# Moving the query transposes of an attention-then-FFN kernel from TensorE to the DMA crossbar, in a layout where two neighbouring tokens share the partitions

## The chip, the cores and the metric

The kernel runs on one core of one Trainium2 chip. The metric is the device time of that core in microseconds (us). Each kernel was run on the same chip beside the kernel before. "Span" is the length of the profiled execution, about 1.8 us shorter than the time. "Granted clock" is the TensorE clock that the profile shows as granted, as a share of full speed.

In this kernel TensorE does the matmuls and, before the change, all transposes; VectorE and ScalarE copy, scale and combine its results; SyncE and GpSimd (POOL) issue the DMAs. SBUF is the on-chip memory that the loads fill, PSUM the one that TensorE writes to. A crossbar transpose is a DMA instruction (`dma_start_transpose`) that writes what it reads transposed.

## The reference

Linformer attention over 8 batches, 8 heads, 1024 tokens and head width 64, followed by a gated FFN over all 8192 tokens:

```python
k_proj = np.einsum('ks,bhsd->bhkd', E, k)          # 1024 tokens -> 64 rows
v_proj = np.einsum('ks,bhsd->bhkd', F, v)
scores = scale * np.matmul(q, k_proj.transpose(0, 1, 3, 2))
attn = exp(scores) / sum(exp(scores))               # the kernel leaves the maximum out
x = np.matmul(attn, v_proj)                         # -> (8192, 512)
gate = 1.0 / (1.0 + np.exp(-(x @ w_gate)))
out = (gate * (x @ w_val)) @ w_out                  # d_ff = 1536, all arrays float32
```

## The kernel before

A small planner records every operation with the tiles it reads and writes; each engine then runs its own list in order and waits on semaphores only. TensorE runs the FFN of batch b and, woven in between, the "pieces" of the attention of batch b + 1.

```python
        def load_kvq(b):                     # POOL queue; casts float32 to bf16 on the way
            s = b % 2
            for t, d, n in ((Kb, k, "K"), (Vb, v, "V"), (Qb, q, "Q")):
                load(t[s][:, :, :],
                     d[b].rearrange("h (p t) d -> p h (t d)", t=NT), [(n, s)], f"{n}{s}")
            # partition p holds tokens 8p .. 8p+7 of each head; t is the token in it
# ... cut ...
            def qt(r):                       # transpose the queries of heads 2r and 2r+1
                bk = next_bank()
                ob = bank[bk][:, :].bitcast(BF16)
                for t in range(NT):
                    for h in range(2):       # 16 transposes in 128x64 tiles
                        mm(bk, ob[64 * h : 64 * h + 64, t * P : (t + 1) * P],
                           Qb[s][:, 2 * r + h, t * DH : (t + 1) * DH],
                           ident[:, :], [("Q", s), "ident"], tr=True, tp=(0, 64 * h))
                dve(lambda e: e.tensor_copy(qT[:, r, :], ob[:, :]), [], [("qT", r)], b=bk)
# ... cut: sc(r) two scores of heads 2r, 2r+1; den, rec, split: 1/sum; bc(c): broadcast it ...
            def xo(c):                       # output: block-diagonal V of two heads
                r, hf = c // 2, c % 2
                bk = next_bank()
                mm(bk, bank[bk][:, :], vpBD[:, r, :], aT[c % 2][:, :], [...])
                act(xT[s][:, r, hf * 512 : (hf + 1) * 512], bank[bk][:, :], [], [...], b=bk)
# ... cut ...
        for piece in attention(0):
            piece()
        load_kvq(1)
        load(wO[:, :, :], moe_w_out.rearrange("(m p) c -> p m c", p=P), ["wO"], "wO")
        for b in range(B):
            pieces = attention(b + 1) if b + 1 < B else []
            todo = list(slots(b))            # 24 FFN steps, and 8 output blocks (4 in batch 0)
            n, done = len(todo) - 1, 0
            for i, slot in enumerate(todo):
                slot()
                while done < len(pieces) and done * n < (i + 1) * len(pieces):
                    pieces[done](); done += 1
            # ... cut: the rest of the pieces; load_kvq(b + 2) ...
```

The attention of batch 0 comes before the first FFN step. Weights and inputs all pass through one load queue, in the order K, V, Q of batch 0, the gate and value weights, K, V, Q of batch 1, wO, K, V, Q of batch 2.

The softmax here doesn't subtract the row's maximum and nothing guards it: scores larger than these inputs give would overflow.

Of the kernel before, what the change touches and what calls it, by code (L numbers as in the profile page):

```python
# [7 lines left out]
ALU = mybir.AluOpType  # L8
# [4 lines left out]
P = 128  # L13
# [106 lines left out]
def bass_linformer_attn__then__ffn_glu_sigmoid_kernel(  # L120
# [18 lines left out]
    with contextlib.ExitStack() as es:  # L139
# [28 lines left out]
        kpBD = sbuf("kpBD", [P, NR, P], BF16)  # L168
        vpBD = sbuf("vpBD", [P, NR, P], BF16)
        qT = sbuf("qT", [P, NR, S], BF16)  # L170
        eT = sbuf("eT", [P, NR, 2, 512], BF16)
        aT = [sbuf(f"aT{i}", [P, 512], BF16) for i in range(2)]
# [3 lines left out]
        xT = [sbuf(f"xT{i}", [P, NI, S], BF16) for i in range(2)]  # L176
# [62 lines left out]
        def constants():  # L239
# [9 lines left out]
            pool(lambda e: e.memset(kpBD[:, :, :], 0.0), w=["kpBD0", "kpBD1"])  # L249
            pool(lambda e: e.memset(vpBD[:, :, :], 0.0), w=["vpBD0", "vpBD1"])  # L250
# [84 lines left out]

        def attention(b):
# [3 lines left out]
            def kv():  # L340
                bk = next_bank()
                for src, wt, c0, n in ((Kb[s], ET, 0, "K"), (Vb[s], FT, 256, "V")):
                    sv = src[:, :, :].rearrange("p (r h) (t d) -> p h t r d", h=2, t=NT)
                    for t in range(NT):
                        for h in range(2):
                            mm(
                                bk,
                                bank[bk][64 * h : 64 * h + 64, c0 : c0 + 256],
                                wt[:, t, :],
                                sv[:, h, t, :, :],  # L350
                                [(n, s), ("ET" if n == "K" else "FT")],
                                start=(t == 0),
                                stop=(t == NT - 1),
                                tp=(0, 64 * h),
                            )
                act(kp[:, :, :], bank[bk][:, 0:256], [], ["kp"], b=bk)
                for h in range(2):
                    hh = slice(64 * h, 64 * h + 64)
                    act(
                        vpBD[hh, :, hh],  # L360
                        bank[bk][hh, 256:512].rearrange("p (r d) -> p r d", r=NR),
                        [],
                        [f"vpBD{h}"],
                        b=bk,
                    )

            def kt():
                bk = next_bank()
                ob = bank[bk][:, :].bitcast(BF16)
                for r in range(NR):  # L370
                    for h in range(2):
                        mm(
                            bk,
                            ob[64 * h : 64 * h + 64, r * P : (r + 1) * P],
                            kp[:, r, :],
                            ident[:, :],
                            ["kp", "ident"],
                            tr=True,
                            tp=(0, 64 * h),
                        )  # L380
                for h in range(2):
                    hh = slice(64 * h, 64 * h + 64)
                    act(
                        kpBD[hh, :, hh],
                        ob[hh, 0:512].rearrange("p (r c) -> p r c", r=NR)[:, :, hh],
                        [],
                        [f"kpBD{h}"],
                        b=bk,
                    )

            def qt(r):
                bk = next_bank()
                ob = bank[bk][:, :].bitcast(BF16)
                for t in range(NT):
                    for h in range(2):
                        mm(
                            bk,
                            ob[64 * h : 64 * h + 64, t * P : (t + 1) * P],
                            Qb[s][:, 2 * r + h, t * DH : (t + 1) * DH],
# [3 lines left out]
                            tp=(0, 64 * h),  # L403
                        )
                dve(lambda e: e.tensor_copy(qT[:, r, :], ob[:, :]), [], [("qT", r)], b=bk)  # L405

            def sc(r):
                for hf in range(2):
                    bk = next_bank()
                    mm(  # L410
                        bk,
                        bank[bk][:, :],
                        kpBD[:, r, :],
                        qT[:, r, hf * 512 : (hf + 1) * 512],
                        ["kpBD0", "kpBD1", ("qT", r)],
                    )
                    act(
                        eT[:, r, hf, :],
                        bank[bk][:, :],
                        [],  # L420
                        [("eT", r, hf)],
                        b=bk,
                        func=AF.Exp,
                        scale=SCALE,
                    )

            def den():
                bk = next_bank()
                st["den"] = bk
                for rnd in range(2):  # L430
                    for j in range(4):
                        r, hf = 2 * rnd + j // 2, j % 2
# [4 lines left out]
                            eT[:, r, hf, :],  # L437
                            ["dsel", ("eT", r, hf)],
# [26 lines left out]
            def bc(c):  # L465
                r, hf = c // 2, c % 2
                rnd, j = r // 2, 2 * (r % 2) + hf
                bk = next_bank()
                mm(bk, bank[bk][:, :], bsel[:, j, rnd, :], rhl[:, :], ["bsel", "rhl"])
                dve(  # L470
                    lambda e: e.tensor_tensor(  # L471
                        aT[c % 2][:, :], eT[:, r, hf, :], bank[bk][:, :], ALU.mult
                    ),
                    [("eT", r, hf)],
                    [("aT", c % 2)],
# [3 lines left out]
            def xo(c):  # L479
                r, hf = c // 2, c % 2  # L480
                bk = next_bank()
                mm(
                    bk,
                    bank[bk][:, :],
                    vpBD[:, r, :],
                    aT[c % 2][:, :],
                    ["vpBD0", "vpBD1", ("aT", c % 2)],
                )
                act(
                    xT[s][:, r, hf * 512 : (hf + 1) * 512],  # L490
                    bank[bk][:, :],
                    [],
                    [("xT", s, r, hf)],
                    b=bk,
                )

            out = [kv, lambda: qt(0), kt, lambda: qt(1)]
            out += [lambda: sc(0), lambda: qt(2), lambda: sc(1), lambda: qt(3)]
            out += [lambda: sc(2), lambda: sc(3), den]
            out += [lambda c=c: rec(c) for c in range(4)] + [split]  # L500
            out += [lambda: bc(0)]
            for c in range(1, 8):
                out += [lambda c=c: (bc(c), xo(c - 1))]
            out += [lambda: xo(7)]
# [5 lines left out]
        def mstep(blk, m):  # L510
# [3 lines left out]
            for W, pb, n in ((wG, PG[M % 2], "wG"), (wV, PV[M % 2], "wV")):  # L514
                for i in range(NI):
# [4 lines left out]
                        xT[s][:, i, hf * 512 : (hf + 1) * 512],  # L520
# [28 lines left out]
        def oproj(blk, tt, pb):  # L549
            T = 4 * blk + tt  # L550
            for m in range(NF):
# [18 lines left out]
                lambda e: e.dma_start(out_v[blk // 2, 4 * (blk % 2) + tt], o[:, :]),  # L570
# [18 lines left out]
        load_kvq(1)  # L589
        load(wO[:, :, :], moe_w_out.rearrange("(m p) c -> p m c", p=P), ["wO"], "wO")  # L590
        for b in range(B):
# [6 lines left out]
            n, done = len(todo) - 1, 0  # L598
            for i, slot in enumerate(todo):
                slot()  # L600
                while done < len(pieces) and done * n < (i + 1) * len(pieces):
# [5 lines left out]
            if load_next is not None:  # L607
                load_kvq(load_next)
# [33 lines left out]
```

## Time and profile before

| | before |
|---|---|
| time, median (range) of the 4 runs | 628.91 us (628.47 to 630.4) |
| period of a full batch on TensorE | 73.11 us |
| one group of query transposes, as delay of the next FFN matmul | 0.654 us |
| four groups a batch, seven batches | 18.3 us |

From the page of the kernel before: its span, the busy row of TensorE and the chain of work that ended last, by engine and by line.

```profile
span 627.3 us, 8171 instructions
PE 589.8 (94%) x3344; PEld 274.7 (44%) x3408; DVE 275.8 (44%) x413; ACT 204.5 (33%) x363; POOL 32.4 (5%) x60
...
PE 88%; DMA 6%; POOL 2%; DVE 2%; issue 1%; ACT 1%; DVEq 0%; POOLq 0%
```

TensorE (PE) is the bound. The 6% of DMA are the load of batch 1's queries at the start, which landed at 54.0 us.

From TensorE's timeline before: start, length, instruction and count. The first three lines are one query group between two FFN matmul groups; the last three show the old output product between a broadcast and the FFN.

```profile
189.33 1.03 PE L202 MATMUL pV<-xT,wV 128*128 128x512 bf16 x4
190.28 0.64 PE L202 MATMUL pA<-ident,Qb 128*64 128x128 bf16 x16
190.85 1.04 PE L202 MATMUL pG<-xT,wG 128*128 128x512 bf16 x4
...
161.67 0.38 PE L202 MATMUL pA<-rhl,bsel 128*128 128x512 bf16 x1
161.89 0.38 PE L202 MATMUL pA<-aT,vpBD 128*128 128x512 bf16 x1
162.10 1.03 PE L202 MATMUL pG<-xT,wG 128*128 128x512 bf16 x4
```

Lengths include the pipeline's tail, so read starts. A 512-column matmul starts 0.216 us after the one before it (161.67, 161.89, 162.10). Four of them from 189.33 end their turn at 190.196; the next FFN matmul starts at 190.85. The query group therefore costs 0.654 us.

From the same timeline, the first projection of K in the attention of batches 1, 2 and 7, which mark where the batches begin:

```profile
45.58 1.06 PE L202 MATMUL pA<-Kb,ET 128*64 128x256 bf16 x16
113.47 1.06 PE L202 MATMUL pA<-Kb,ET 128*64 128x256 bf16 x16
479.02 1.06 PE L202 MATMUL pA<-Kb,ET 128*64 128x256 bf16 x16
```

The period is (479.02 - 113.47) / 5 = 73.11 us.

### The profile page before, as it was taken

To read this page: it belongs to the slowest core of one execution; us is meant where nothing else is said; L and a number is where in the kernel's file an instruction comes from. 1 tells how busy PE (TensorE), PEld (TensorE's weight loads), DVE (VectorE), ACT (ScalarE), POOL (GpSimd) and SP (SyncE) were. 2 spreads that over 40 slices of the span, in tenths; PEclk is the share of its full clock that TensorE was granted. 3 is DMA by queue.
4 is the path that set the end of the run, shared out by engine and by line. 5 is a ranking of instruction groups with operands and counts; after the bars stand their busy time and mean duration, and the time that the engine had idled before them with its cause. 6 is when DMAs were issued, how large, how long until landed. Compare 5 with 4: busy or idle time off the path is not lost.

```text
span 627.3 us, 8171 instructions
## 1 busy us (share of the span) xinstructions
PE 589.8 (94%) x3344; PEld 274.7 (44%) x3408; DVE 275.8 (44%) x413; ACT 204.5 (33%) x363; POOL 32.4 (5%) x60
## 2 busy tenths in 40 slices
PE   2558999999999999999999999999999999999997
PEld 1313444544444444544445444444445444444443
DVE  2162465336543365334653365433653346533332
ACT  1333424232333324333242323333243332422220
POOL 8301000100001000100001000000000000000000
PEclk9978999999999999999999999999999999999999
DMA  9999990652009500375006620000000000000002
GB/s 138 207 207 207 207 175 34 113 106 67 34 35 152 101 34 19 63 138 85 34 34 111 114 62 34 34 18 33 34 24 27 34 18 34 34 34 33 34 33 84
DMA packets 39092, 47.44 MB, mean 76 GB/s; under 512 B 1552, under 2 KB 30736, under 8 KB 39056
## 3 DMA queue, kind: packets, MB, share of 16 engines
q0 software_dynamic: 29840, 30.15, 30.4%
q1 hardware_dynamic: 9216, 16.78, 7.2%
q8 instruction: 26, 0.43, 0.3%
q14 instruction: 10, 0.08, 0.0%
HBM read 60.29 MB, written 16.78 MB: 123 GB/s over the span
## 4 chain that ended last, share of the span: by engine, by line
PE 88%; DMA 6%; POOL 2%; DVE 2%; issue 1%; ACT 1%; DVEq 0%; POOLq 0%
PE pG L202 26%; PE pO L202 25%; PE pV L202 25%; PE pA L202 12%; DMA Qb<-in_q_dram 6%; DVE ost L563 1%; DVE aT L471 1%; ACT sig L206 1%; POOL wG L221 0%; POOL dsel L258 0%; POOL wV L221 0%; POOL Kb L221 0%; POOL Vb L221 0%; POOL bsel L251 0%; POOL Qb L221 0%
## 5 line engine op out<-in xcount | busy, mean ns | idle before, releaser
L536 DVE SCALAR_TENSOR_TENSOR hT<-sig,pV 128x512 bf16<-128x512 f32 x192 | 132.1, 688 | 211.4 <-PE pV L202 207.2
L202 PE MATMUL pG<-xT,wG 128*128 128x512 bf16 x750 | 195.4, 380 | 2.2 <-issue 1.4
L202 PE MATMUL pV<-xT,wV 128*128 128x512 bf16 x746 | 195.7, 380 | 0.8
L206 ACT ACTIVATE sig<-pG 128x512 f32<-128x512 f32 x192 | 114.8, 598 | 246.1 <-PE pG L202 231.7
L202 PE MATMUL pO<-wO,hT 128*128 128x512 bf16 x717 | 166.1, 379 | 2.3 <-issue 1.0
L202 PEld LDWEIGHTS pV<-xT,wV 128*128 128x128 bf16 x768 | 75.4, 98 | 91.2 <-issue 1.1
L202 PEld LDWEIGHTS pG<-xT,wG 128*128 128x128 bf16 x768 | 72.2, 98 | 88.2 <-issue 4.4
L202 PEld LDWEIGHTS pO<-wO,hT 128*128 128x128 bf16 x732 | 70.6, 98 | 85.8 <-DVE ost L563 1.3
L563 DVE TENSOR_SCALAR ost<-pO 128x512 f32<-128x512 f32 x61 | 42.2, 692 | 104.4 <-PE pO L202 104.4
L206 ACT ACTIVATE xT<-pA 128x512 bf16<-128x512 f32 x64 | 38.3, 598 | 68.2 <-PE pA L202 68.0
L206 ACT ACTIVATE eT<-pA 128x512 bf16<-128x512 f32 x64 | 34.7, 596 | 48.5 <-PE pA L202 48.5
L471 DVE TENSOR_TENSOR aT<-eT,pA 128x512 bf16<-128x512 bf16 x64 | 43.5, 681 | 2.1 <-PE pA L202 2.0
L448 DVE RECIPROCAL rden<-pA 128x128 f32<-128x128 f32 x32 | 30.0, 946 | 2.1 <-PE pA L202 2.1
L405 DVE COPY qT<-pA 128x1024 bf16<-128x1024 bf16 x32 | 22.1, 690 | 18.2 <-PE pA L202 18.2
L202 PE MATMUL pA<-rhl,bsel 128*128 128x512 bf16 x58 | 23.0, 400 | 6.2 <-DVE rhl L458 5.0
L202 PE MATMUL pA<-ident,Qb 128*64 128x128 bf16 x512 | 21.5, 229 | 4.3 <-DMA Qb<-in_q_dram 4.0
L202 PE MATMUL pA<-aT,vpBD 128*128 128x512 bf16 x63 | 24.4, 387 | 0.8 <-DVE aT L471 0.7
L202 PEld LDWEIGHTS pA<-ident,Qb 128*64 128x64 bf16 x512 | 16.2, 114 | 18.4 <-issue 11.4
L202 PE MATMUL pA<-qT,kpBD 128*128 128x512 bf16 x63 | 19.1, 384 | 0.8 <-ACT kpBD L206 0.5
L221 POOL DMA_DIRECT2D Kb<-in_k_dram x8 | 7.2, 899 | 217.6 <-PE pA L202 217.6
L202 PE MATMUL pA<-Kb,ET 128*64 128x256 bf16 x128 | 9.4, 294 | 6.7 <-DMA Kb<-in_k_dram 6.7
L202 PE MATMUL pA<-Vb,FT 128*64 128x256 bf16 x128 | 9.2, 292 | 5.5 <-DMA Vb<-in_v_dram 5.5
(53 smaller groups left out, 119.3 us busy)
## 6 DMA issues: line engine op xcount, KB each, us to landing
out_dram<-ost SPq DMA_DIRECT2D x64, 256.0 KB, 2.0
Kb<-in_k_dram POOLq DMA_DIRECT2D x8, 1024.0 KB, 9.8
Vb<-in_v_dram POOLq DMA_DIRECT2D x8, 1024.0 KB, 14.6
Qb<-in_q_dram POOLq DMA_DIRECT2D x8, 1024.0 KB, 13.9
wG<-in_moe_w_gate_dram POOLq DMA_DIRECT2D x3, 512.0 KB, 19.4
wV<-in_moe_w_val_dram POOLq DMA_DIRECT2D x3, 512.0 KB, 21.2
wO<-in_moe_w_out_dram POOLq DMA_DIRECT2D x1, 1536.0 KB, 44.3
Ebf<-in_E_dram POOLq DMA_DIRECT2D x1, 128.0 KB, 2.9
```

What stands on the lines that cost most here:

```text
L202: return add("PE", lambda e: e.matmul(o, lhsT, rhs, **kw), r=r, x=[("bank", b)])
L206: return add("ACT", lambda e: e.activation(o, i, func, scale=scale), r=r, w=w, x=x)
L221: add("POOL", lambda e: e.dma_start(o, i), r=r, w=w, dma=sem)
L405: dve(lambda e: e.tensor_copy(qT[:, r, :], ob[:, :]), [], [("qT", r)], b=bk)
L448: lambda e: e.reciprocal(rden[:, cc], bank[bk][:, cc]),
L471: lambda e: e.tensor_tensor(aT[c % 2][:, :], eT[:, r, hf, :], bank[bk][:, :], ALU.mult),
L536: lambda e: e.scalar_tensor_tensor(hT[blk % 2][:, m, :], sg[:, :], 1.0, bank[PV[M % 2]][:, :], ALU.add, ALU.mult,),
L563: lambda e: e.tensor_scalar(o[:, :], bank[pb][:, :], 0.5, None, op0=ALU.mult),
```

## The change

The intent is to take the query transposes, and the copies out of PSUM behind them, off the compute engines. Batches 1 to 7 get their transposed queries from four crossbar transposes each, issued on SyncE's queue from SBUF to SBUF. Such a transpose turns 128 columns of Qb at a time into 128 partitions, and 128 columns are two neighbouring tokens of 64 values: so the transposed queries of the even tokens lie in partitions 0 to 63 and those of the odd tokens in 64 to 127. The rest of the attention follows this layout: one head per score matmul, K twice on a diagonal, and the output product as four 64x64 tiles. Batch 0 keeps TensorE, with eight full 128x128 transposes per group.

```diff
+        def transpose_q(b):
+            s = b % 2
+            for r in range(NR):
+                add(
+                    "SP",
+                    lambda e, r=r: e.dma_start_transpose(
+                        qT[s][:, 2 * r : 2 * r + 2, :].rearrange("p h (t c) -> p (h t) c", c=P),
+                        Qb[s][:, 2 * r : 2 * r + 2, :].rearrange("p h c -> p (h c)"),
+                    ),
+                    r=[("Q", s)], w=[("qT", s, r)], dma=f"qT{s}{r}",
+                )
@@ qt: groups of transposes, now for batch 0 only @@
-                for t in range(NT):
-                    for h in range(2):
+                for h in range(2):
+                    for t in range(4):
...
-                            Qb[s][:, 2 * r + h, t * DH : (t + 1) * DH],
+                            Qb[s][:, 2 * r + h, t * P : (t + 1) * P],
@@ the output product @@
-            def xo(c):   # one 128x128 matmul per half, into one bank
+            def xo(r):
+                bks = [next_bank(), next_bank()]
+                for g in range(2):
+                    gg = slice(64 * g, 64 * g + 64)
+                    for c in range(2):
+                        h = 2 * r + c
+                        mm(bks[g], bank[bks[g]][64 * c : 64 * c + 64, :],
+                           vpD[gg, h, :], aT[h % 4][gg, :],
+                           [("vpD", c, g), ("aT", h % 4)], tp=(64 * g, 64 * c))
@@ the order @@
         load_kvq(1)
+        transpose_q(1)
         load(wO[:, :, :], moe_w_out.rearrange("(m p) c -> p m c", p=P), ["wO"], "wO")
...
+            if load_next is not None:
+                load_kvq(load_next)
             for i, slot in enumerate(todo):
                 slot()
+                if i == 16 and load_next is not None:
+                    transpose_q(load_next)
... (cut: the tiles' shapes, sc, den and bc by head, the evictions of K and V, the rows of the output)
```

More of the change, by code (lines that the diff above doesn't have):

```diff
@@ L167, in bass_linformer_attn__then__ffn_glu_sigmoid_kernel @@
         kp = sbuf("kp", [P, NR, DH], BF16)
-        kpBD = sbuf("kpBD", [P, NR, P], BF16)
-        vpBD = sbuf("vpBD", [P, NR, P], BF16)
-        qT = sbuf("qT", [P, NR, S], BF16)
-        eT = sbuf("eT", [P, NR, 2, 512], BF16)
-        aT = [sbuf(f"aT{i}", [P, 512], BF16) for i in range(2)]
+        kpBD = sbuf("kpBD", [P, H, P], BF16)
+        vpD = sbuf("vpD", [P, H, DH], BF16)
+        qT = [sbuf(f"qT{i}", [P, H, 512], BF16) for i in range(2)]
+        eT = sbuf("eT", [P, H, 512], BF16)
+        aT = [sbuf(f"aT{i}", [P, 512], BF16) for i in range(4)]
         rden = sbuf("rden", [P, 512], FP32)
@@ L175, in bass_linformer_attn__then__ffn_glu_sigmoid_kernel @@
         rhl = sbuf("rhl", [P, 512], BF16)
-        xT = [sbuf(f"xT{i}", [P, NI, S], BF16) for i in range(2)]
+        xT = [sbuf(f"xT{i}", [P, NI, 2, 512], BF16) for i in range(2)]
         wG = sbuf("wG", [P, NI, DFF], BF16)
@@ L248, in constants @@
             )
-            pool(lambda e: e.memset(kpBD[:, :, :], 0.0), w=["kpBD0", "kpBD1"])
-            pool(lambda e: e.memset(vpBD[:, :, :], 0.0), w=["vpBD0", "vpBD1"])
+            pool(lambda e: e.memset(kpBD[:, :, :], 0.0), w=[("kpBD", 0), ("kpBD", 1)])
             pool(lambda e: e.memset(bsel[:, :, :, :], 0.0), w=["bsel"])
@@ L334, in next_bank @@
             return b
+        def transpose_q(b):
[7 more added lines that the diff above has]
+                    ),
+                    r=[("Q", s)],
+                    w=[("qT", s, r)],
+                    dma=f"qT{s}{r}",
+                )
         def attention(b):
@@ L356, in kv @@
                 act(kp[:, :, :], bank[bk][:, 0:256], [], ["kp"], b=bk)
+                vv = vpD[:, :, :].rearrange("p (r h) d -> p r h d", h=2)
                 for h in range(2):
-                    hh = slice(64 * h, 64 * h + 64)
-                    act(
-                        vpBD[hh, :, hh],
-                        bank[bk][hh, 256:512].rearrange("p (r d) -> p r d", r=NR),
-                        [],
-                        [f"vpBD{h}"],
-                        b=bk,
-                    )
+                    for g in range(2):
+                        act(
+                            vv[64 * g : 64 * g + 64, :, h, :],
+                            bank[bk][64 * h : 64 * h + 64, 256:512].rearrange(
+                                "p (r d) -> p r d", r=NR
+                            ),
+                            [],
+                            [("vpD", h, g)],
+                            b=bk,
+                        )
             def kt():
@@ L370, in kt @@
                 for r in range(NR):
-                    for h in range(2):
+                    for g in range(2):
                         mm(
                             bk,
-                            ob[64 * h : 64 * h + 64, r * P : (r + 1) * P],
+                            ob[64 * g : 64 * g + 64, r * P : (r + 1) * P],
                             kp[:, r, :],
@@ L378, in kt @@
                             tr=True,
-                            tp=(0, 64 * h),
+                            tp=(0, 64 * g),
                         )
-                for h in range(2):
-                    hh = slice(64 * h, 64 * h + 64)
-                    act(
-                        kpBD[hh, :, hh],
-                        ob[hh, 0:512].rearrange("p (r c) -> p r c", r=NR)[:, :, hh],
+                for g in range(2):
+                    gg = slice(64 * g, 64 * g + 64)
+                    act(
+                        kpBD[gg, :, gg],
+                        ob[gg, 0:512].rearrange("p (h c) -> p h c", h=H),
                         [],
-                        [f"kpBD{h}"],
+                        [("kpBD", g)],
                         b=bk,
@@ L393, in qt @@
                 ob = bank[bk][:, :].bitcast(BF16)
-                for t in range(NT):
-                    for h in range(2):
-                        mm(
-                            bk,
-                            ob[64 * h : 64 * h + 64, t * P : (t + 1) * P],
-                            Qb[s][:, 2 * r + h, t * DH : (t + 1) * DH],
+                for h in range(2):
+                    for t in range(4):
+                        c = h * 4 + t
+                        mm(
+                            bk,
+                            ob[:, c * P : (c + 1) * P],
+                            Qb[s][:, 2 * r + h, t * P : (t + 1) * P],
                             ident[:, :],
@@ L402, in qt, with sc @@
                             tr=True,
-                            tp=(0, 64 * h),
                         )
-                dve(lambda e: e.tensor_copy(qT[:, r, :], ob[:, :]), [], [("qT", r)], b=bk)
-            def sc(r):
-                for hf in range(2):
-                    bk = next_bank()
-                    mm(
-                        bk,
-                        bank[bk][:, :],
-                        kpBD[:, r, :],
-                        qT[:, r, hf * 512 : (hf + 1) * 512],
-                        ["kpBD0", "kpBD1", ("qT", r)],
-                    )
-                    act(
-                        eT[:, r, hf, :],
-                        bank[bk][:, :],
-                        [],
-                        [("eT", r, hf)],
-                        b=bk,
-                        func=AF.Exp,
-                        scale=SCALE,
-                    )
+                dve(
+                    lambda e: e.tensor_copy(
+                        qT[s][:, 2 * r : 2 * r + 2, :].rearrange("p h c -> p (h c)"), ob[:, :]
+                    ),
+                    [],
+                    [("qT", s, r)],
+                    b=bk,
+                )
+            def sc(h):
+                bk = next_bank()
+                mm(
+                    bk,
+                    bank[bk][:, :],
+                    kpBD[:, h, :],
+                    qT[s][:, h, :],
+                    [("kpBD", 0), ("kpBD", 1), ("qT", s, h // 2)],
+                )
+                act(
+                    eT[:, h, :],
+                    bank[bk][:, :],
+                    [],
+                    [("eT", h)],
+                    b=bk,
+                    func=AF.Exp,
+                    scale=SCALE,
+                )
             def den():
@@ L431, in den @@
                     for j in range(4):
-                        r, hf = 2 * rnd + j // 2, j % 2
+                        h = 4 * rnd + j
                         mm(
@@ L436, in den @@
                             dsel[:, rnd, :],
-                            eT[:, r, hf, :],
-                            ["dsel", ("eT", r, hf)],
+                            eT[:, h, :],
+                            ["dsel", ("eT", h)],
                             start=(rnd == 0),
@@ L463, in split, with bc @@
                 )
-            def bc(c):
-                r, hf = c // 2, c % 2
-                rnd, j = r // 2, 2 * (r % 2) + hf
+            def bc(h):
                 bk = next_bank()
-                mm(bk, bank[bk][:, :], bsel[:, j, rnd, :], rhl[:, :], ["bsel", "rhl"])
+                mm(bk, bank[bk][:, :], bsel[:, h % 4, h // 4, :], rhl[:, :], ["bsel", "rhl"])
                 dve(
                     lambda e: e.tensor_tensor(
-                        aT[c % 2][:, :], eT[:, r, hf, :], bank[bk][:, :], ALU.mult
+                        aT[h % 4][:, :], eT[:, h, :], bank[bk][:, :], ALU.mult
@@ L473, in bc @@
                     ),
-                    [("eT", r, hf)],
-                    [("aT", c % 2)],
+                    [("eT", h)],
+                    [("aT", h % 4)],
                     b=bk,
                 )
-            def xo(c):
-                r, hf = c // 2, c % 2
-                bk = next_bank()
-                mm(
-                    bk,
-                    bank[bk][:, :],
-                    vpBD[:, r, :],
-                    aT[c % 2][:, :],
-                    ["vpBD0", "vpBD1", ("aT", c % 2)],
-                )
-                act(
-                    xT[s][:, r, hf * 512 : (hf + 1) * 512],
-                    bank[bk][:, :],
-                    [],
-                    [("xT", s, r, hf)],
-                    b=bk,
-                )
@@ L497, in attention @@
-            out = [kv, lambda: qt(0), kt, lambda: qt(1)]
-            out += [lambda: sc(0), lambda: qt(2), lambda: sc(1), lambda: qt(3)]
-            out += [lambda: sc(2), lambda: sc(3), den]
+            def xo(r):
+                bks = [next_bank(), next_bank()]
+                for g in range(2):
+                    gg = slice(64 * g, 64 * g + 64)
+                    for c in range(2):
+                        h = 2 * r + c
+                        mm(
+                            bks[g],
+                            bank[bks[g]][64 * c : 64 * c + 64, :],
+                            vpD[gg, h, :],
+                            aT[h % 4][gg, :],
+                            [("vpD", c, g), ("aT", h % 4)],
+                            tp=(64 * g, 64 * c),
+                        )
+                for g in range(2):
+                    act(xT[s][:, r, g, :], bank[bks[g]][:, :], [], [("xT", s, r, g)], b=bks[g])
@@ L500, in attention @@
+            out = [kv]
+            if b == 0:
+                out += [lambda r=r: qt(r) for r in range(2)]
+            out += [kt]
+            if b == 0:
+                out += [lambda r=r: qt(r) for r in range(2, 4)]
+            out += [lambda h=h: sc(h) for h in range(H)] + [den]
             out += [lambda c=c: rec(c) for c in range(4)] + [split]
-            out += [lambda: bc(0)]
-            for c in range(1, 8):
-                out += [lambda c=c: (bc(c), xo(c - 1))]
-            out += [lambda: xo(7)]
+            out += [lambda: bc(0), lambda: bc(1)]
@@ L505, in attention @@
+            for r in range(1, 4):
+                out += [lambda r=r: bc(2 * r), lambda r=r: (xo(r - 1), bc(2 * r + 1))]
+            out += [lambda: xo(3)]
             return out
@@ L519, in mstep @@
                         W[:, i, m * P : (m + 1) * P],
-                        xT[s][:, i, hf * 512 : (hf + 1) * 512],
+                        xT[s][:, i, hf, :],
                         [(n, j), ("xT", s, i, hf)],
@@ L569, in oproj @@
                 "SP",
-                lambda e: e.dma_start(out_v[blk // 2, 4 * (blk % 2) + tt], o[:, :]),
+                lambda e: e.dma_start(out_v[blk // 2, 2 * tt + blk % 2], o[:, :]),
                 r=[("ost", T % 4)],
@@ L606, in bass_linformer_attn__then__ffn_glu_sigmoid_kernel @@
                 done += 1
-            if load_next is not None:
-                load_kvq(load_next)
         last = 2 * B - 1
```

## The prediction

> **What bounds the kernel.** TensorE. It is busy 94% of the 627.3 us span (busy table), its granted clock is 0.99, and the chain that ended last is 88% TensorE. By the windows view the six full batches take 73.1 us each with 72.5 us busy, and in the timeline 128x512 matmuls start 216 ns apart. ScalarE and VectorE are busy 25 and 34 us of such a batch: they have slack. Before 54 us the load queue bounds (DMA full, chain: queries of batch 1 land at 54.0); it stays full until 91 us.
>
> **Removed from TensorE.** Per batch four groups of 16 query transposes. In the timeline one group delays the next FFN matmul by 0.654 us (190.196 to 190.85): about 0.45 of work and 0.2 of entering and leaving the 128x64 tiling. "Mode switching requires drain" (the Trainium skill, TensorEngine Tiling (Array Packing), Key Properties) agrees: the denominators, also tiled, cost 0.644, of which 0.43 is work. So 4 x 0.654 = 2.6 us a batch, 18.3 us over batches 1 to 7, all on the critical path. VectorE loses 28 copies of 0.69 us, off the path.
>
> **Changed on TensorE.** The output product: 8 full matmuls a batch (1.73 us) become 4 groups of four 64x64 tiles. If all four tiles of a group overlap, a group costs 0.216 + 0.2 of switching: nothing is gained or lost. The trace shows overlap of column tiles (16 matmuls of 256 columns in 0.90 us), none of row tiles; if only pairs overlap, 32 groups lose 0.216 us each: +7 us. Scores, denominators, broadcasts and projections keep their count. ScalarE gets two more 64x256 evictions of 0.37 us a batch, off the path.
>
> **Added.** 28 crossbar transposes of 256 KB on SyncE's queue, which the output stores share. No trace times one. Estimates: 1 us at the 261 GB/s of the Trainium skill (DMA: Bandwidth & Descriptors, Latency and other measured facts), 10.5 us as eight times the 1309 ns for 128x128 of VectorE: DVE Perf Modes, The three transpose paths. I expect 3 to 5 us each when the queues are quiet. In steady state they are issued at slot 16 of 32, about 35 us before the first score that needs them, beside few loads: hidden, unless one takes over about 9 us; then stores queue behind them, the four output buffers (31 us) run out and TensorE stalls in each of six batches.
>
> **Where part is given back.** Batch 1's queries land at 54.0 while the queue is still full; then four transposes run in turn beside the loads (a 256 KB store took 2.0 us in quiet, up to 6.7 beside loads), and TensorE, in order, stops at the first score at about 55.6. Without that stop TensorE would be ahead here by one FFN step and the key transpose, 2.1 us, besides 2.6. I expect the last of these waits to cost 8 to 10 us in all, once.
>
> **Sum.** 629 - 18.3 - 2.1 + 9 = about 617.5 us, range 609 to 634. Chances: faster by over 2% 0.42, within 2% 0.44, slower by over 2% 0.14.
>
> **What would show it.** Batch period 73.1 to about 70.5 us (72.5 - 73 would mean that tiles overlap only in pairs); waits of TensorE for the transposed queries only between 54 and 85 us, 5 to 12 us in all; the four matmuls of an output group within 0.25 us; landing of a transpose 3 to 5 us in the DMA issues; no wait of VectorE for output stores.
>
> **What would make it wrong.** Transposes several times slower than estimated (slower kernel, waits in each batch); their landing quick even beside the loads (609); row tiles that don't overlap, or a dearer switch with row tiles; the clock falling during the first wait.

## The result and the profile after

| | before | after |
|---|---|---|
| time, median (range), 4 runs each | 628.91 us (628.47 to 630.4) | 629.2 us (628.31 to 630.33) |
| ratio, 95% interval | | 1.0001 (0.9978 to 1.0025) |
| period of a full batch | 73.11 us | 70.47 us |
| start of the projection of batch 2 | 113.47 us | 128.40 us |

Ratios are the mean time of one kernel's runs over that of the other's of the same rounds, so not quite the ratio of the medians. The time is the same as before, where 617.5 us were predicted. Nearly all of the predicted gain of the steady state is there, and nearly all of it is given back at the start.

From the page after: the same lines as above.

```profile
span 626.5 us, 7388 instructions
PE 579.2 (92%) x2936; PEld 260.7 (42%) x2992; DVE 258.0 (41%) x385; ACT 211.7 (34%) x379; POOL 32.4 (5%) x59
...
PE 85%; DMA 9%; SPq 2%; POOL 2%; issue 1%; DVE 1%; DVEq 0%; POOLq 0%
```

The chain has less TensorE and more DMA; SPq, the queue that issues the transposes, is new in it. The chain in order of time after, from the start of batch 1's query load (start, length, what), shows where:

```profile
16.39 36.34 DMA Qb<-in_q_dram
...
52.76 1.34 SPq L340
...
67.11 18.13 DMA qT<-Qb
...
85.29 0.39 PE pA L202
```

The queries land at 52.74 us, SyncE issues their four transposes (line 340), and TensorE goes on at 85.29 us, when the fourth has landed. The waits of TensorE after (total, times, longest):

```profile
PE pA L202 <- DMA qT<-Qb: 15.6, 3, 9.5
```

The batches after, by the same marker as before:

```profile
48.26 1.70 PE L202 MATMUL pA<-Kb,ET 128*64 128x256 bf16 x16
128.40 1.06 PE L202 MATMUL pA<-Kb,ET 128*64 128x256 bf16 x16
480.76 1.06 PE L202 MATMUL pA<-Kb,ET 128*64 128x256 bf16 x16
```

The markers cut the span into four stretches that add up:

| stretch | before, us | after, us | difference |
|---|---|---|---|
| start to batch 1's projection | 45.58 | 48.26 | +2.68 |
| batch 1's projection to batch 2's | 67.89 | 80.14 | +12.25 |
| five full periods | 365.55 | 352.36 | -13.19 |
| batch 7's projection to the end | 148.28 | 145.74 | -2.54 |
| span | 627.3 | 626.5 | -0.8 |

The second row can be taken apart with the timelines. The waits of TensorE for loads and transposes in it grow from 3.13 us (V 2.30, Q 0.83) to 15.64: +12.51. The query groups of batch 1 are gone: -2.62. Stretches at a lower granted clock cost about 2.1 us more than before, as an estimate from the spacing of the matmuls (about 3.5 us after, 1.4 before). The sum is 12.0 of 12.25. The clock is seen in the timeline after, at the end of the first wait (the bracket is the idle time before and its releaser):

```profile
52.94 1.04 PE L202 MATMUL pG<-xT,wG 128*128 128x512 bf16 x4
53.81 1.03 PE L202 MATMUL pV<-xT,wV 128*128 128x512 bf16 x4
64.33 0.59 PE L202 MATMUL pA<-qT,kpBD 128*128 128x512 bf16 x1 [9.49 <-DMA qT<-Qb]
64.70 1.91 PE L202 MATMUL pG<-xT,wG 128*128 128x512 bf16 x4
66.41 1.91 PE L202 MATMUL pV<-xT,wV 128*128 128x512 bf16 x4
```

Four FFN matmuls start 0.87 us apart before the wait (52.94 to 53.81) and 1.71 us apart after it (64.70 to 66.41). In the windows view the granted clock is 0.50 from 64 to 66 us. The work from 64.33 to 70.17 us takes 5.84 us; at the pace before the wait it would take 3.0.

The 2.68 us of the first row are a lower clock too: the first FFN step starts 0.97 us later and takes 3.44 us instead of 1.73. The clock falls in both kernels while TensorE waits 4.7 us for the first reciprocals, but it is back at about 40 us before and only at about 49 us after. All runs with the new layout except e9 have it low until 47 us or later. Why it comes back later there was not tested. In the kernel after this costs nothing by itself, as its chain runs here through the query load and the transposes and not through TensorE: had TensorE come earlier, it would have waited longer for the same transposes. Where that wait is taken away, this delay remains.

The last lines are one transpose instruction after: the four of batch 1 between 50 and 100 us, then the four of batch 3 in a stretch without loads. Each pair gives the time on the issuing queue in ns, then the time from issue to landing in us, as lowest, median and highest.

```profile
L340 SPq DMA_TRANSPOSE qT<-Qb x4: 1343/6432/6890, 52.8 to 67.1; - x4
DMA to landing us min/median/max: 11.4/17.4/18.1
...
L340 SPq DMA_TRANSPOSE qT<-Qb x4: 1275/1280/1288, 163.9 to 168.0; - x4
DMA to landing us min/median/max: 3.2/3.2/3.3
```

The same instruction lands after 3.2 us in quiet and after 11.4 to 18.1 us here. During the four of batch 1 the load queue still carries wO and K, V, Q of batch 2. That is the theory to test: the loads make them slow. The rivals are that the first transposes are slow by themselves, that the new order or layout of the attention is what costs time in batch 1, and that the clock is the cause and not a consequence.

The output product came out as predicted. From the timeline after:

```profile
109.03 1.03 PE L202 MATMUL pV<-xT,wV 128*128 128x512 bf16 x4
109.99 0.41 PE L202 MATMUL pA<-aT,vpD 64*64 64x512 bf16 x4
110.33 0.39 PE L202 MATMUL pA<-rhl,bsel 128*128 128x512 bf16 x1
```

The FFN's turn ends at 109.03 + 4 x 0.216 = 109.90 and the broadcast starts at 110.33: 0.43 us for the group of four tiles with both switches, against 2 x 0.216 before. One after the other, four such matmuls would take 0.86 us, so the tiles overlap; the group gains and loses nothing.

### The profile page after: what moved, and what is told of

Read it like the earlier page. It is cut to its first block, busy times and chain, and to the rows that moved or that the text cites. A ratio compares the mean times of both kernels' runs of the same rounds, so it can differ in the third digit from the quotient of the medians.

```text
span 626.5 us, 7388 instructions
## 1 busy us (share of the span) xinstructions
PE 579.2 (92%) x2936; PEld 260.7 (42%) x2992; DVE 258.0 (41%) x385; ACT 211.7 (34%) x379; POOL 32.4 (5%) x59
## 3 DMA queue, kind: packets, MB, share of 16 engines
q0 software_dynamic: 29840, 30.15, 29.8%
## 4 chain that ended last, share of the span: by engine, by line
PE 85%; DMA 9%; SPq 2%; POOL 2%; issue 1%; DVE 1%; DVEq 0%; POOLq 0%
PE pV L202 25%; PE pO L202 25%; PE pG L202 25%; PE pA L202 10%; DMA Qb<-in_q_dram 6%; DMA qT<-Qb 3%; SPq L340 2%; POOL wG L221 0%; POOL dsel L257 0%; POOL Kb L221 0%; POOL wV L221 0%; POOL Vb L221 0%; DVE ost L586 0%; POOL kpBD L249 0%; POOL bsel L250 0%
## 5 line engine op out<-in xcount | busy, mean ns | idle before, releaser
L206 ACT ACTIVATE eT<-pA 128x512 bf16<-128x512 f32 x64 | 37.5, 601 | 75.6 <-PE pA L202 75.6
L206 ACT ACTIVATE xT<-pA 128x512 bf16<-128x512 f32 x64 | 34.7, 594 | 43.7 <-PE pA L202 43.7
L202 PE MATMUL pA<-qT,kpBD 128*128 128x512 bf16 x63 | 24.3, 388 | 16.5 <-DMA qT<-Qb 15.6
L202 PE MATMUL pA<-rhl,bsel 128*128 128x512 bf16 x64 | 25.9, 412 | 5.2 <-DVE rhl L480 5.0
L202 PEld LDWEIGHTS pA<-qT,kpBD 128*128 128x128 bf16 x64 | 6.3, 98 | 26.5 <-issue 10.2
L202 PE MATMUL pA<-aT,vpD 64*64 64x512 bf16 x128 | 15.8, 429 | 0.2
L202 PEld LDWEIGHTS pA<-rhl,bsel 128*128 128x128 bf16 x64 | 6.2, 98 | 17.5 <-DVE rhl L480 5.8
L206 ACT ACTIVATE kp<-pA 128x256 bf16<-128x256 f32 x8 | 3.1, 384 | 28.5 <-PE pA L202 28.5
L206 ACT ACTIVATE vpD<-pA 64x256 bf16<-64x256 f32 x32 | 12.0, 375 | 0.6
```

The costliest lines, as they stand in the source:

```text
L202: return add("PE", lambda e: e.matmul(o, lhsT, rhs, **kw), r=r, x=[("bank", b)])
L206: return add("ACT", lambda e: e.activation(o, i, func, scale=scale), r=r, w=w, x=x)
```

## The experiments

Ten kernels were run, e1 to e10. All start from the kernel after, except e4. Ratios are to the kernel before in the same rounds (median 629.0 to 630.8 us).

### e3: hold the competing loads back

```diff
-        load(wO[:, :, :], moe_w_out.rearrange("(m p) c -> p m c", p=P), ["wO"], "wO")
+        load(wO[:, :, :], moe_w_out.rearrange("(m p) c -> p m c", p=P), ["wO"], "wO",
+             r=[("qT", 1, r) for r in range(NR)])
```

> The kernel after, but the load of wO, and so those of batch 2 behind it in the same queue, waits until the four transposes of batch 1 have landed; nothing else changes. Theory (contention with the loads makes the first transposes slow): they land in about 3.3 us each instead of 11 to 18, SyncE issues one in 1.3 us instead of 6.4, the waits of TensorE for transposed queries fall from 15.6 to under 2 us, the clock does not fall at 64 us, and the time is 609 to 613 us. Rival (the first transposes are slow by themselves, or SyncE is late, whatever else is loaded): landing stays at 11 us or more, time 627 to 630. A rest of loss may come if wO or batch 2 now arrive too late.

Measured: 611.59 us, ratio to before 0.9708 (0.9683 to 0.9733). TensorE's wait for transposed queries, and the four transposes of batch 1 (here the last two of them):

```profile
PE pA L202 <- DMA qT<-Qb: 1.3, 1, 1.3
```

```profile
L340 SPq DMA_TRANSPOSE qT<-Qb x2: 1325/1334/1343, 56.1 to 57.5; - x2
DMA to landing us min/median/max: 3.3/3.4/3.5
```

The same four instructions on the same data, with the same FFN and attention around them, land after 3.2 to 3.5 us. Nothing but the time of other loads was changed. So the first transposes are not slow by themselves, and the layout and order of batch 1's attention are not what cost the time. The granted clock from 54 to 64 us is 1.00, where it fell after: the fall was a consequence of the wait. The transposes of batch 2 now run beside loads and take 6.7 to 17.6 us, but they are issued 20 us or more ahead of their use and nobody waits.

### e1: leave batch 1 on TensorE as well

```diff
-            if b == 0:
+            if b <= 1:
                 out += [lambda r=r: qt(r) for r in range(2)]        # and the same for range(2, 4)
...
-        transpose_q(1)
```

> The kernel after, with the queries of batch 1 also transposed on TensorE (in the paired layout); batches 2 to 7 keep the crossbar. Theory: the crossbar gains 2.64 us in each of batches 2 to 7 and gives all of it back once, in batch 1, whose transposes run beside the tail of the load queue. Then the time is 629 - 6 x 2.64 - about 0.9 (groups of full 128x128 transposes without a switch of tiling) = about 612.5 us (611 to 615), and no wait for transposed queries is left. Rival A, the loss comes from the new order or layout of the attention in batch 1 (one score per slot, two banks per output group): about 625 to 629. Rival B, the loss comes from the colder clock at the end of batch 0's attention (FFN starts at 44.7 instead of 43.8 us): about 617 or more.

Measured: 614.7 us, ratio 0.9755 (0.9726 to 0.9783). This is inside the expected range and excludes both rivals: with batch 1 off the crossbar, the gain of the other six batches stands (their period is 70.47 us). It is 2 us above the point value. TensorE waits 3.1 us for the load of batch 1's queries itself, but that cannot explain it, since the kernel before waits 3.13 us there for batch 1's V and Q. What the estimate left out is the delay in batch 0: batch 1's projection starts at 48.60 us, against 45.58 before, after the longer stretch at the low clock.

### e2: the new layout without the crossbar

```diff
-            if b == 0:
+            if True:                                  # every batch transposes on TensorE
...
-        transpose_q(1)
...
-                if i == 16 and load_next is not None:
-                    transpose_q(load_next)
```

> The kernel after with no crossbar transpose at all: every batch on TensorE, in the paired layout, 8 full 128x128 transposes per group instead of 16 in 128x64 tiles. If the layout alone saves the switch of tiling (about 0.2 us of the 0.65 of a group), the period is 73.1 - 0.9 = about 72.2 us and the time about 622.5 (621 to 625). If the crossbar alone makes the gain (rival): 628 to 630, period 73.1.

Measured: 626.78 us, ratio 0.9948 (0.9919 to 0.9978), period 72.68 us: slower than the expected 621 to 625 us, faster than the rival's 628 to 630. One query group in its timeline:

```profile
196.74 1.03 PE L202 MATMUL pV<-xT,wV 128*128 128x512 bf16 x4
197.60 0.61 PE L202 MATMUL pA<-ident,Qb 128*128 128x128 bf16 x8
198.05 1.03 PE L202 MATMUL pG<-xT,wG 128*128 128x512 bf16 x4
```

A group now costs 0.445 us (197.605 to 198.05) and not 0.654. The transposes are now in the tiling of the FFN's matmuls, and half as many; I put the difference down to the change of tiling, but no run separates the two. Four groups should save 0.84 us a batch, but the period fell by 0.43. A new wait of 0.25 us a batch, of the first broadcast for the reciprocals, takes part of it back, probably because the four query pieces push the reciprocals one slot further. The remaining 0.16 us I did not find. The delay in batch 0 is here too: batch 1's projection starts at 49.45 us. So of the 2.64 us a batch, the layout alone gives about 0.4, and freeing TensorE of the groups altogether gives the rest.

### e4: the kernel before with a later start of batch 1's attention

```diff
-                while done < len(pieces) and done * n < (i + 1) * len(pieces):
+                k0 = 5 if b == 0 else 0
+                while done < len(pieces) and done * (n - k0) < (i + 1 - k0) * len(pieces):
```

> The kernel before, with the attention of batch 1 begun only at slot 5 of the first FFN pass instead of slot 0 (control: how much of any gain of a later start belongs to the start and not to the transposes). Its waits for V (2.3) and Q (0.8) of batch 1 and about 1.4 us of cold clock at 50 to 53 us should go: about 624.5 us (623 to 626.5). If those waits were hidden by something else: 629.

Measured: 625.35 us, ratio 0.9924 (0.99 to 0.9947), as expected. The old kernel, too, lost time at this place, by asking for batch 1's inputs before they had landed; this control keeps that gain apart from the crossbar's.

### e5: hold the loads and start late

The edits of e3 and e4 together.

> The kernel after with both: the loads of wO and batch 2 held until batch 1's transposes have landed (as in e3_hold_loads), and batch 1's attention begun at slot 5 of the first FFN pass (as in e4_before_late). Theory: after the hold only 1.3 us of waits for transposed queries are left, and the late start removes them: 609 to 611 us, one or two below the 611.6 of e3. If the late start is worth as much here as on the kernel before (4.8 us): about 607. If it crowds the attention into too few slots: above 612.

Measured: 610.16 us, ratio 0.9703 (0.9681 to 0.9725). The wait for transposed queries is gone. The interval overlaps that of e3, so the late start's own share on top of the hold is not shown.

### e7: the rival remedy

The edits of e1 and e4 together.

> Batch 1 on TensorE as in e1_b1_on_pe (614.7 us) and its attention begun at slot 5: the 3.2 us that it waited for Q of batch 1 go, and some cold clock: about 610 to 612 us, so equal to holding the loads. This is the rival remedy to e5_hold_late.

Measured: 612.36 us, ratio 0.9737 (0.9717 to 0.9758); 0.4 us above what was expected. Keeping batch 1 on TensorE is nearly as good as holding the loads; the interval overlaps that of e5.

### e6: every steady-state transpose four times

```diff
+            if b >= 2:
+                for c in range(3):
+                    for r in range(NR):
+                        add("SP", lambda e, r=r: e.dma_start_transpose(<qX[r]>, <Qb[s] as above>),
+                            r=[("Q", s)], w=[("qX", r)], dma=f"qX{r}")      # nobody reads qX
```

> The kernel after, with each crossbar transpose of batches 2 to 7 issued four times (three copies into tiles that nothing reads). Theory (in steady state the crossbar is hidden, with room to spare): the period stays 70.47 us and the time 628 to 631, as the kernel after; SyncE is taken for some 21 us a batch and one or two output stores come late without TensorE noticing. Rival (the crossbar or its SBUF traffic costs TensorE something in each batch): the period grows with the copies, by over 0.3 us.

Measured: 629.31 us, ratio 1.0003 (0.9979 to 1.0027). Two neighbouring batches in its timeline, and the copies:

```profile
200.06 1.06 PE L203 MATMUL pA<-Kb,ET 128*64 128x256 bf16 x16
270.53 1.06 PE L203 MATMUL pA<-Kb,ET 128*64 128x256 bf16 x16
```

```profile
L354 SPq DMA_TRANSPOSE qX<-Qb x72: 1309/1335/2272, 108.1 to 467.6; - x72
DMA to landing us min/median/max: 3.2/3.4/5.3
```

The period is 70.47 us with sixteen transposes a batch as with four. In steady state the crossbar costs TensorE nothing that can be seen, with room for four times as much. That the first wait is as long as in the kernel after (9.5 us) is the same loss again.

### e8 and e10: how a transpose and a load share an engine

The Trainium skill (DMA: Bandwidth & Descriptors, Queues, rings and completion order) states that a DMA engine goes round-robin between its queues "at *packet* granularity". If so, what slows a transpose is the size of the load packets it takes turns with. The passage gives a packet as several descriptors, "≈9-17 descriptors typical", while the profile counts one packet for each row of a load here; whether the two are the same thing is not shown. In what follows a packet is what the profile counts. The queue lines of the page, q1 before, then q0 (the loads) and q1 (SyncE) after, with packets, MB and share:

```profile
q1 hardware_dynamic: 9216, 16.78, 7.2%
...
q0 software_dynamic: 29840, 30.15, 29.8%
q1 hardware_dynamic: 38784, 24.12, 14.2%
```

The 29568 more packets in SyncE's queue are 28 transposes of 1056, or 66 on each of 16 engines per transpose, of about 250 bytes (7.34 MB in all). The loads of wO and K, V, Q of batch 2 are 4608 rows of 1 KB.

e8 loads these 4608 rows in 512 long ones (the order of the data is wrong on purpose):

```diff
-                    t[s][:, :, :],
-                    d[b].rearrange("h (p t) d -> p h (t d)", t=NT),
+                    t[s][:, :, :].rearrange("p h c -> p (h c)"),             # for b == 2 only
+                    d[b].rearrange("h (x y) d -> (h x) (y d)", x=16),        # for b == 2 only
...
-        load(wO[:, :, :], moe_w_out.rearrange("(m p) c -> p m c", p=P), ["wO"], "wO")
+        load(wO[:, :, :].rearrange("p m c -> p (m c)"),
+             moe_w_out.rearrange("(p m) c -> p (m c)", p=P), ["wO"], "wO")
```

> The kernel after with wO and the K, V, Q of batch 2 loaded in long rows (6144 and 4096 elements in one run per partition, instead of runs of 512), the same bytes; the result is wrong on purpose (rows are permuted). It asks how the engines share time between a transpose and a load. If they take turns packet by packet, a 256-byte packet of the transpose waits for a whole load packet: 66 packets per engine and transpose beside 1 KB packets of 0.10 us each make the 6.4 us per issue of the kernel after; beside packets several times longer the transposes of batch 1 take several times longer (issue 15 to 50 us), and the kernel is slower by 20 us or more. If they share by bytes, or the long rows are cut to packets of the same size: issue about 6.4 us, landing 11 to 18, time 627 to 631. If the loads themselves get quicker with long rows, the contention ends earlier: 615 to 625.

e10 loads them in 9216 short rows, as two half-width DMAs for each load (the result is correct):

```diff
+        def load_halves(o, i, key, sem):        # o, i: the two halves of 256 columns
+            first = load(o[0], i[0], [key], sem)
+            second = load(o[1], i[1], [("second", key)], sem + "b")
+            second.deps += first.deps
+            plan.writers[key].append(second)    # a reader of key waits for both
```

> The mirror of e8_long_rows: in the kernel after, wO and the K, V, Q of batch 2 are loaded in runs of 256 elements instead of 512 (two DMAs for each, the same bytes, the result stays correct), so twice as many load packets of half the size. If engines take turns packet by packet, the 264 transpose packets of an engine meet 264 short ones, which carry half the bytes: the transposes of batch 1 end after about 46% of these loads instead of 92%, issue falls from 6.4 to about 4 us, the last landing from 85 us to 70-75, and TensorE's waits for transposed queries from 15.6 to under 9 us. If they share by bytes: issue 6 us or more, waits about 15 us.

Measured: e8 637.72 us (a single look, its state unknown; wrong result, as meant); e10 620.42 us, ratio 0.9843 (0.9788 to 0.9897; two runs, and unclear by the 2% verdict). The load queue's packets, TensorE's wait, and the landings of batch 1's transposes, first e8 (its four transposes), then e10 (its last two):

```profile
q0 software_dynamic: 25744, 30.15, 28.6%
...
PE pA L202 <- DMA qT<-Qb: 25.8, 1, 25.8
```

```profile
L342 SPq DMA_TRANSPOSE qT<-Qb x4: 1342/5412/21068, 54.0 to 83.0; - x4
DMA to landing us min/median/max: 10.0/20.1/31.6
```

```profile
q0 software_dynamic: 34512, 30.15, 31.5%
...
PE pA L202 <- DMA qT<-Qb: 8.9, 1, 8.9
```

```profile
L355 SPq DMA_TRANSPOSE qT<-Qb x2: 4151/4154/4158, 59.1 to 63.3; - x2
DMA to landing us min/median/max: 12.6/13.2/13.7
```

The bytes are the same (30.15 MB in this queue), the packets are not: 25744 in e8 and 34512 in e10, against 29840 in the kernel after. With long rows TensorE waits 25.8 us for the first transpose, with short ones 8.9 us, and in between 15.6. Sharing by bytes would have left all three alike.

The sizes fit turns, as an estimate. In the kernel after, the four transposes take 85.2 - 52.8 = 32.5 us, so one of an engine's 264 turns takes 0.123 us. At the 207 GB/s that the GB/s row of the page shows while only loads run, an engine's share of a 1 KB packet is 0.079 us, which leaves 0.044 for the transpose's own packet. With 512-byte packets a turn should take 0.040 + 0.044, and 264 of them 22.1 us; in e10 the last transpose landed 23.3 us after the first issue (63.3 + 13.7 - 53.7). In e8 the first transpose's 66 packets meet an engine's 32 long rows, that is all of the 4608 KB (22.8 us), and 34 ordinary turns of K and V of batch 3 (4.2 us), 27.0 us together; it landed after 26.2. Several expectations of mine within this pair were off. I expected e8 to be slower by 20 us or more; it took 8.5 us more than the kernel after, in keeping with 10.2 us more of waiting, because only the first transpose was waited for. In e8's issue times I expected all to be longer, but only one is much longer, at 21 us. In e10 the last transpose landed at 77.0 us and not at 70 to 75, and the shares "46% instead of 92%" left out that K and V of batch 3 queue behind batch 2's loads. What is shown is that the rows' length decides, in this pair of runs; the turns themselves are inferred.

### e9: keep TensorE busy in batch 0's attention

Matmuls whose result nobody reads, in the 4.7 us in which TensorE waits for the first reciprocals, on top of e5:

```diff
             out += [lambda c=c: rec(c) for c in range(4)] + [split]
+            if b == 0:
+                out += [lambda: mm(PO, bank[PO][:, :], ident[:, :], Kb[0][:, 0, :],
+                                   [("K", 0), "ident"]) for _ in range(28)]
```

> The version e5_hold_late (610.2 us) with 28 matmuls whose result nobody reads, put on TensorE between the split of the reciprocals' issue and batch 0's first broadcast, where it idles for 4.7 us: they keep it busy while VectorE computes the reciprocals. In e5 the granted clock is 0.50 from 36 to 44 us and 0.65 from 44 to 50, and the first FFN step takes about 3.4 us instead of 1.7. If the clock falls because of that idle stretch, it now stays near 1.0 from 36 us on, and the time is about 607.5 us (606 to 609). If the clock does not follow these matmuls: 610. If they run into the broadcasts (more than 4.7 us at a low clock): 611 to 613.

Measured: 609.77 us, ratio 0.9691 (0.9667 to 0.9716). The granted clock is now 1.00 from 30 us on, where e5 had 0.50 from 36 to 44 us, so the idle stretch was what lowered it. The time is inconclusive: the interval overlaps that of e5. In the trace batch 1's projection starts 1.2 us earlier (56.16 against 57.37). It could have been more: the 28 matmuls take 6.1 us, longer than the wait that they fill, so the first broadcast starts 1.1 us later than in e5 (37.92 against 36.78). From there to the first FFN step it is 7.68 us at the full clock, 8.93 in e5, 8.92 in the kernel after and 7.83 in the kernel before, so the 0.97 us by which that step was late after the change come from the clock as well.

## Why the prediction was wrong

- **The bound, the cost of a query group, and the steady gain: right.** TensorE was the bound, a group cost 0.654 us, and the period fell by 2.64 us for a predicted 2.6. "18.3 us over batches 1 to 7" is what came off TensorE's work.
- **The output product: right.** "nothing is gained or lost": 0.43 us a group against 0.432.
- **A transpose in quiet: right.** Predicted 3 to 5 us, measured 3.2; e6 shows that it is hidden, and no output store held anything up.
- **The step that failed** is the term "I expect the last of these waits to cost 8 to 10 us in all, once". The place and the mechanism (the queries of batch 1 land while the load queue is full, and TensorE stops in order) were right; the size was not. TensorE waited 15.6 us, and lost about 2.8 us more at half clock after the first wait, which the sum left out although the text named it as a risk. The credit of 2.1 us for being ahead was not seen either: TensorE came to batch 1 2.7 us late, at a low clock, for which the prediction had no term.
- **Why it was mis-sized.** I scaled a 256 KB output store, which went from 2.0 to 6.7 us beside loads, about 3 times. The transpose of the same bytes goes from 3.2 to 11.4 us and more, and four in a row to 32.5 us. It is cut into 1056 packets, where a store has 144 (9216 for 64), and e8 and e10 show that the wait grows with the rows of the loads beside it. That each packet takes its turn with a load packet four times its size fits these runs and is inferred.
- The sum was therefore 617.5 where 629.2 was measured: the give-back at the start is 12.25 + 2.68 us in the span and not the 4.3 (9 - 2.1 - 2.6) that the prediction put there.

Both e1 and e3 show that nothing else of this size was wrong: take away the contention, or the use of the crossbar at that one place, and 14 to 18 us appear. What stays hidden behind the wait, and is left in e1 (48.60 us) and e3 (48.91), is the delay in batch 0, about 3 us.

## What to carry to other kernels

A change that is hidden in the steady state has to be checked where the pipeline fills: there the queues are full, nothing is ahead, and one slow first use can cost as much as the steady state gains in all other rounds. Beside bulk loads, look at a DMA's packets, and at the rows of the loads, and not only at its bytes. The remedy here was one added dependency: let loads that are not yet needed wait until the small transfer on the critical path has landed (629.2 to 611.6 us in e3, 610.2 with a later start in e5).

## What the Trainium skill lacked or had wrong

- DMA: Bandwidth & Descriptors: its rule that "A transpose next to ordinary DMAs needs nothing" is about correctness, and the results here were indeed correct; no page says what the loads cost it in time. A 256 KB SBUF-to-SBUF transpose landed after 3.2 us in quiet and after 11.4 to 18.1 us beside loads with 1 KB packets, 26.2 to 31.6 us for the first two beside long rows (e8).
- The same page, Queues, rings and completion order: the turns at packet granularity fit these runs, if the profile's packets of one row each are the packets meant; that the share of an engine then goes by packet size, so that the row length of one load sets the speed of another queue's transfer, isn't drawn out. TensorE's wait was 8.9, 15.6 and 25.8 us with short, middle and long rows of the same bytes.
- VectorE: DVE Perf Modes, The three transpose paths: 1309 ns for a 128x128 transpose is no rate. Eight such blocks in one instruction landed after 3.2 us, and one instruction followed another every 1.3 us (e6).
- TensorEngine Tiling (Array Packing), Key Properties: says that a change of tiling drains TensorE but not what it costs. Here entering and leaving together cost about 0.2 us (0.654 us a tiled group against 0.445 us in full tiles, of the same data), if the whole difference is the change of tiling.
